# Chunks of 64 tokens and loads by token in a retention and feed-forward kernel

## The chip, the cores and the metric

The kernel runs on one core of a Trainium2 chip. The metric is the device time of one execution in microseconds (us). The profile is one execution, recorded by the hardware profiler.

## The reference

Retention over 4 sequences of 768 tokens, 8 heads, head size 64, then a feed-forward layer with a leaky activation over all 3072 tokens:

```python
for t in range(S):
    state = gamma[None, :, None, None] * state + np.einsum('bhd,bhe->bhde', k[:, :, t], v[:, :, t])
    y[:, :, t] = scale * np.einsum('bhd,bhde->bhe', q[:, :, t], state)
...
h = x @ w_in
g = np.maximum(h, 0.0) + alpha * np.minimum(h, 0.0)
return (g @ w_out).astype(np.float32)
```

`x` is y with its heads side by side (3072 x 512), `w_in` is 512 x 2048 and `w_out` 2048 x 512. Everything comes and goes in float32.

## The kernel before

**Blocks, units, loads.** The feed-forward layer works in six blocks of 512 tokens (n from 0 to 5). A block of retention is two units of 256 tokens and 8 heads (u from 0 to 11, three to a sequence). A unit is loaded as two parts (w = 2u and 2u + 1), each 4 heads by 256 tokens: three DMAs of 256 KB (k, q, v), in which a partition holds two neighbouring tokens of a head, 512 bytes in one piece (`load`, L151). `prep` (L183 to L212) scales k and q by powers of the decay on GpSimd into float16 (`scaled`, L191), casts v (L211), and from w = 8 on turns k and q by one DMA transpose (L204) into `kq`, with the head dimension on the partitions. For w = 0 to 7 TensorE does the turning.

**Retention in chunks.** Before the change a chunk is 128 tokens. Inside a chunk the products of q and k (scores, into PSUM) are masked on VectorE into float16 (`m2`) and multiplied with v ("inner", L360 in `inner`). What comes from earlier chunks is the product of q with a running state `tgs` ("carried", L340 in `carried`). The state is brought forward on VectorE by adding the chunk's sum of k times v (L511) and multiplying by the decay of 128 tokens (L513). All these matmuls use a quarter of the array each, 64 rows by 64 columns, four of them beside each other; their moving operand has 128 columns for scores, inner and carried, and 64 for the state sums (L481).

**Visits.** From block 2 on retention is done in visits of TensorE between matmuls of the feed-forward layer. `both(u_old, u_new)` (L425) does the last steps of an old unit and the first steps of a new one: scores of the new unit's second part into spare halves of banks (`low`, `sums`, L437), a small VectorE instruction that tells when they are through (`through`, L372), inner and half of carried for the old unit, a small ScalarE instruction (`word`, L374) that tells when these are through, scores of the first part, state sums, the other half of carried (it writes the bank that the other row half wrote before, so it waits for `word`), then on ScalarE the copy of y to `xT` (L498), and masks and states on VectorE.

**The order around them is written by hand.** For block n, `ffn1` (matmuls L557, 64 of them, activation on ScalarE L537 and VectorE L526) and `ffn2` (matmuls L582, four groups of 16, copies L596, stores L602) are generators; `tick(gen, m)` lets m matmuls go by. L754 to L774 interleave: two or four calls of `ahead()` in `ffn1`, then in `ffn2(n)` the visits. In block n = 1 there are three: (none, 4) after 8 matmuls, (4, 5) 28 later, (5, 6) 21 later. Then, 20 and 53 matmuls into `ffn2`: (6, 7) and (7, 8) at n = 2, (8, 9) and (9, 10) at n = 3, (10, 11) and (11, none) at n = 4. `ahead()` does `prep(w)` and then `load(w + 4)`, from w = 8 on.

**Queues.** Loads, transposes and stores are all issued by SyncE, in program order. GpSimd does casts and scalings in program order. `Banks` (L109) gives the order in which `ffn1` goes through the eight PSUM banks: f and p are two banks each that alternate, s and y pairs (S and Y their second halves). `ffn2` uses the f banks alone; `both` uses s, y and the p banks (`pa`, `pb`), and before the change an f bank for `low`.

Of the kernel before, what the change touches and what calls it, by code (L numbers as in the profile page):

```python
# [18 lines left out]
def kernel(  # L19
# [14 lines left out]

    nc = tc.nc
# [24 lines left out]
    for g in range(2):  # L60
        for x in range(2):
            for r in range(2):
                tab_np[64 * r : 64 * r + 64, 32 + 2 * g + x] = g64[4 * g + 2 * r + x] ** 128
    ALT = 48
# [8 lines left out]
    mi_np[:, 256:384] = np.eye(128)  # L73

# [9 lines left out]
    mask = mi[:, 0:256]  # L84
    ident = mi[:, 256:384]
# [59 lines left out]
    def load(w, which="kqv"):  # L145
        u, g, b, c3 = place(w)
        t = staged.setdefault(w, {})
        for nm in which:
            src = {"k": k, "q": q, "v": v}[nm]
            t[nm] = sbp.tile([128, 4, 2 * D], FP, tag=f"{nm}s", bufs=8, name=f"{nm}s{w}")  # L150
            nc.sync.dma_start(  # L151
                out=t[nm],
                in_=src[b, 4 * g : 4 * g + 4, TU * c3 : TU * c3 + TU, :].rearrange(
                    "h (p a) d -> p h (a d)", a=2
                ),
            )
# [26 lines left out]
    def prep(w, opening=False, k_on=None, q_on=None):  # L183
        u, g, b, c3 = place(w)
        t = staged.pop(w)
        kdq = sbp.tile([128, 2, 4, 2, D], F16, tag="kdq", bufs=8, name=f"kdq{w}")
        vx = sbp.tile([128, 4, 2, D], F16, tag="vx", bufs=8, name=f"vx{w}")
        kq = sbp.tile([128, 8, 128], F16, tag="kq", bufs=8, name=f"kq{w}")

        def scaled(eng, kind, src):  # L190
            eng.tensor_tensor(  # L191
                out=kdq[:, kind].rearrange("p z r d -> p r z d"),
                in0=src.rearrange("p (r x) (a d) -> p r (x a) d", a=2, x=2),
                in1=tab[:, 16 * kind + 8 * g : 16 * kind + 8 * g + 8]
                .rearrange("p (r z) -> p r z", r=2)
                .unsqueeze(3)
                .to_broadcast([128, 2, 4, D]),
                op=MULT,
            )
# [12 lines left out]
        prepped[w] = (kdq, kq, vx)  # L212
# [86 lines left out]

    def masked(w):  # L300
        kdq, kq, vx, sc = live[w]
        m2 = sbp.tile([128, 4, 2, 128], F16, tag="m2", bufs=4, name="m2")
# [8 lines left out]
    def new_state():  # L311
        return sbp.tile([128, 4, D], F16, tag="tg", bufs=8, name="tg")

    def state(w, cs=None):
        u, g, b, c3 = place(w)
        decay = tab[:, 32 + 2 * g : 34 + 2 * g].unsqueeze(2).to_broadcast([128, 2, D])
        for c in cs or chunks(w):
# [4 lines left out]
            if 2 * u + c + 1 not in tgs:  # L322
                tgs[2 * u + c + 1] = new_state()
            nc.vector.tensor_tensor(out=tgs[2 * u + c + 1][:, gs], in0=stv, in1=decay, op=MULT)

    def single(g, c, r):
        return slice(256 + 256 * c + 128 * r, 384 + 256 * c + 128 * r)

    def double(g, c, r):
        return slice(512 * c + 256 * g + 128 * r, 512 * c + 256 * g + 128 * r + 128)  # L330

    def carried(w, y, started, same, after=None, at=single):
        u, g, b, c3 = place(w)
        kq = live[w][1]
        for x in range(2):
            for r in range(2):
                c = r if same else 1 - r
                if c3 + c == 0:
                    continue
                ins = nc.tensor.matmul(  # L340
                    out=y[half(x), at(g, c, r)],
# [12 lines left out]
    def inner(w, y, started, at=single):  # L354
        u, g, b, c3 = place(w)
        vx, m2 = live[w][2:4]
        for r in range(2):
            for a in range(2):
                for c, x in DIAG:
                    nc.tensor.matmul(  # L360
                        out=y[half(x), at(g, c, r)],
# [63 lines left out]
    def both(u_old, u_new):  # L425
# [6 lines left out]
        def score(w, at):  # L432
            kq = prepped[w][1]
            for x in range(2):
                for a in range(2):
                    for r, c in DIAG:
                        last = nc.tensor.matmul(  # L437
                            out=at[r][x][half(c), 128 * a : 128 * a + 128],
                            lhsT=kq[half(r), 2 * x + a, half(c)],
                            rhs=kq[half(r), 4 + 2 * x : 6 + 2 * x, half(c)],  # L440
                            start=True,
                            stop=True,
                        )
            return last

        def masks(dst, src):
            nc.vector.tensor_tensor(  # L447
                out=dst.rearrange("p s a i -> p s (a i)"),
                in0=src.rearrange("p (s n) -> p s n", n=256),
                in1=mask.unsqueeze(1).to_broadcast([128, dst.shape[1], 256]),  # L450
                op=MULT,
            )

        if new:
            u, _, b, c3 = place(new[0])
            cs = chunks(new[0])
            low = ps("low", "fb" if flip["f"] else "fa")
            sums = [ps(f"sums{c}", "pa" if c == 0 else "pb") for c in range(2)]
            beside = [t[:, 256:512] for t in sums]
            there = through(score(new[1], ((low[:, 0:256], low[:, 256:512]), beside)))  # L460
            m2 = [sbp.tile([128, 4, 2, 128], F16, tag="m2", bufs=4, name="m2") for _ in new]
            masks(m2[1][:, 0:2], low)
# [8 lines left out]
        if new:  # L471
            sc = ps("sc", "s")
            score(new[0], [[sc[:, 512 * r + 256 * x :][:, 0:256] for x in range(2)] for r in range(2)])
            for w in new:
                kdq, kq, vx = prepped[w]
                for x in range(2):
                    for a in range(2):
                        for c, r in DIAG:
                            if c in cs:
                                at = 128 * (w % 2) + 64 * x  # L480
                                ins = nc.tensor.matmul(  # L481
                                    out=sums[c][half(r), at : at + 64],
                                    lhsT=kdq[half(c), 0, 2 * x + a, r, :],
                                    rhs=vx[half(c), 2 * r + x, a, :],
                                    start=(a == 0),
                                    stop=(a == 1),
                                )
                                if there is not None:
                                    behind(ins, there, "the other row half wrote this bank")
                                    there = None  # L490
        if old:
            for w in old:
                carried(w, y, started, False, done if w == old[0] else None, double)
# [4 lines left out]
            nc.scalar.activation(  # L498
                out=xT[n][:, 4 * i : 4 * i + 4].rearrange("p c r (i a) -> p (c r) i a", a=2),
                in_=y.rearrange("p (s a i) -> p s i a", a=2, i=64),  # L500
# [4 lines left out]
        if new:  # L505
            for c in range(2):
                masks(m2[1][:, 2 + c : 3 + c], beside[c])
            for c in cs:
                stv = sums[c][:, 0:256].rearrange("p (z e) -> p z e", e=D)
                if c3 + c > 0:  # L510
                    nc.vector.tensor_tensor(out=stv, in0=tgs[2 * u + c], in1=stv, op=ADD)  # L511
                tgs[2 * u + c + 1] = new_state()
                nc.vector.tensor_tensor(  # L513
                    out=tgs[2 * u + c + 1],
                    in0=stv,
                    in1=tab[:, 32:36].unsqueeze(2).to_broadcast([128, 4, D]),
                    op=MULT,
                )
            masks(m2[0], sc)
            for w, m in zip(new, m2):  # L520
                live[w] = [*prepped.pop(w), m]
# [171 lines left out]
    for w in range(2 * WB, 3 * WB):  # L693
        load(w)
# [42 lines left out]
    visit(6, 7, None, ("pb", "fa"))  # L737
    tick(gen, 4)
# [5 lines left out]
    more = [8]  # L744

    def ahead():
        w = more[0]
        if w < NW:
            prep(w)
            if w + WB < NW:  # L750
                load(w + WB)
            more[0] += 1

    for n in range(1, NBLK):  # L754
        gen = ffn1(n, "fyfpsYpS" if n > 1 else "spyfSpYf")
        for i in range(4 if n == 1 else 2):
            tick(gen, 14 if n == 1 else 20)
# [5 lines left out]
        if n + 1 < NBLK:  # L763
            tick(gen, 8)
            if n == 1:
# [39 lines left out]
```

## Time and profile before

| what | value |
| --- | --- |
| time, median of 3 runs | 210.86 us (210.62 to 211.15) |
| the profiled execution: its own time | 211.09 us |
| its span, first to last instruction | 209.1 us |
| TensorE matmuls busy | 201.5 us (96%), 2135 of them |
| VectorE, ScalarE, GpSimd busy | 123.2, 97.9, 72.8 us |
| granted TensorE clock | 0.998 |
| DMA moved | 38.27 MB in 64119 packets, 64.6% of 16 engines' span on SyncE's queue |

The profile's chain of waits tells which work ended last, step by step; its pieces are start, length, engine, name and line, and how many instructions were merged. The chain starts a matmul's piece where the one before has ended, so its pieces add up to the span. The groups give the busy time of a line, where the matmuls' modelled ends overlap. Queue and wait views tell what an engine or the DMA queue of SyncE waited for.

### The profile page before, as it was taken

Reading aid. Unit: us, or ns where it says so; the run is one execution under the profiler, and the core shown is the slowest. Engines: PE = TensorE matmul, PEld = TensorE weight load, DVE = VectorE, ACT = ScalarE, POOL = GpSimd, SP = SyncE. Lnnn points to the kernel's source line nnn. Section 1 sums busy time; section 2 is a strip of 40 time slices with the busy share of each in tenths; the row PEclk is TensorE's granted clock in tenths of the full one; section 3 lists DMA queues with packets and bytes.
Section 4 is the critical chain, followed back from the end, with each engine's and each line's share of the span. In section 5 each row is a group of like instructions: output and inputs, shape, how many; then the busy total and the mean of one; then the engine's idle time right before and its main releaser. Section 6 shows DMA issues by size and latency. Waiting matters only on the chain.

```text
span 209.1 us, 5197 instructions
## 1 busy us (share of the span) xinstructions
PE 201.5 (96%) x2135; PEld 101.5 (49%) x2135; DVE 123.2 (59%) x209; ACT 97.9 (47%) x166; POOL 72.8 (35%) x97
## 2 busy tenths in 40 slices
PE   7988999999999999999999999999999999999993
PEld 2565445445444555444555444545444544444452
DVE  2583886557588834888373688354888340588000
ACT  2572865174666122666233566233566123665121
POOL 0388798479927664345450054000000000000000
PEclk9999999999999999999999999999999999999999
DMA  6999999999999999799911399111410111100112
GB/s 179 307 286 345 389 389 383 371 312 306 358 254 253 298 252 202 248 233 265 266 71 74 104 235 211 53 56 56 122 31 0 50 53 50 53 0 0 50 55 96
DMA packets 64119, 38.27 MB, mean 183 GB/s; under 512 B 19152, under 2 KB 57568, under 8 KB 64096
## 3 DMA queue, kind: packets, MB, share of 16 engines
q1 hardware_dynamic: 63632, 37.69, 64.6%
q8 instruction: 16, 0.26, 0.5%
q10 hardware_dynamic: 464, 0.25, 0.5%
q14 instruction: 7, 0.06, 0.1%
HBM read 27.45 MB, written 6.29 MB: 161 GB/s over the span
## 4 chain that ended last, share of the span: by engine, by line
PE 88%; SPq 4%; DMA 3%; DVE 1%; ACT 1%; issue 1%; POOL 0%; DVEq 0%; ACTq 0%
PE hps L557 40%; PE ops L582 39%; SPq L151 4%; DMA wi<-in_moe_w_in_dram 3%; PE y L360 2%; PE y L340 2%; PE low L437 1%; PE sums L481 1%; PE sc L437 1%; PE trb L239 1%; DVE m L303 1%; ACT kq L245 0%; PE sc L267 0%; ACT os L596 0%; PE st L292 0%
## 5 line engine op out<-in xcount | busy, mean ns | idle before, releaser
L582 PE MATMUL ops<-wout,gt 128*128 128x512 f16 (+1 forms) x400 | 87.2, 371 | 0.3 <-ACT os L596 0.3
L526 DVE SCALAR_TENSOR_TENSOR gt<-hm,oma,hps 128x512 f16<-128x512 f32 x96 | 71.2, 747 | 26.4 <-ACT hm L537 16.7
L557 PE MATMUL hps<-xT,win 128*128 128x512 f16 (+1 forms) x392 | 84.8, 375 | 0.5 <-POOL win L181 0.5
L537 ACT ACTIVATE hm<-hps 128x512 f32<-128x512 f32 x96 | 57.0, 597 | 24.9 <-PE hps L557 24.5
L557 PEld LDWEIGHTS <-win 128*128 128x128 f16 x392 | 38.0, 98 | 45.3 <-POOL win L181 0.7
L582 PEld LDWEIGHTS <-gt 128*128 128x128 f16 x400 | 37.9, 98 | 41.4 <-issue 0.6
L596 ACT ACTIVATE os<-ops 128x512 f32<-128x512 f32 (+2 forms) x25 | 14.2, 576 | 46.6 <-PE ops L582 46.6
L191 POOL TENSOR_TENSOR kdq<-ks,tab 128x512 f16<-128x512 f32 x19 | 19.8, 1042 | 38.6 <-DMA ks<-in_k_dram 30.5
L191 POOL TENSOR_TENSOR kdq<-qs,tab 128x512 f16<-128x512 f32 x22 | 23.2, 1054 | 9.4 <-DMA ks<-in_k_dram 7.8
L447 DVE TENSOR_TENSOR m<-low,mi 128x512 f16<-128x512 f32 x8 | 5.5, 686 | 24.8 <-issue 24.0
L245 ACT ACTIVATE kq<-trb 128x512 f16<-128x512 f16 (+1 forms) x12 | 8.6, 736 | 10.7 <-PE trb L239 10.6
L211 POOL CAST vx<-vs 128x512 f16<-128x512 f32 x16 | 9.8, 610 | 3.5 <-PE y L360 3.0
L181 POOL CAST win<-wi 128x512 f16<-128x512 f32 x16 | 9.8, 613 | 2.8 <-DMA wi<-in_moe_w_in_dram 2.3
L181 POOL CAST wout<-wo 128x512 f16<-128x512 f32 x16 | 9.6, 613 | 3.3 <-DMA wo<-in_moe_w_out_dram 3.1
L303 DVE TENSOR_TENSOR m<-sc,mi 128x1024 f16<-128x1024 f32 x8 | 9.8, 1222 | 0.8 <-PE sc L267 0.4
L498 ACT ACTIVATE xT<-y 128x1024 f16<-128x1024 f32 x8 | 8.2, 1023 | 3.3 <-PE y L340 3.3
L447 DVE TENSOR_TENSOR m<-sc,mi 128x1024 f16<-128x1024 f32 x8 | 9.7, 1214 | 0.0
L340 PE MATMUL y<-kq,tg 64*64 64x128 f16 x160 | 8.5, 224 | 0.5 <-ACT word L374 0.4
L360 PE MATMUL y<-m,vx 64*64 64x128 f16 x384 | 8.3, 218 | 0.2 <-DVE m L303 0.2
L219 PE MATMUL trb<-ones 128*128 128x512 f16 (+1 forms) x21 | 6.5, 434 | 1.5 <-DVE word L624 1.4
L374 ACT ACTIVATE word<-word 1x1 f32<-1x1 f32 x11 | 2.2, 201 | 12.1 <-PE y L340 12.1
L600 DVE COPY os<-ops 128x128 f32<-128x128 f32 x1 | 0.3, 291 | 12.8 <-ACT os L596 12.8
(39 smaller groups left out, 99.5 us busy)
## 6 DMA issues: line engine op xcount, KB each, us to landing
ks<-in_k_dram SPq DMA_DIRECT2D x24, 256.0 KB, 4.6
qs<-in_q_dram SPq DMA_DIRECT2D x24, 256.0 KB, 4.7
vs<-in_v_dram SPq DMA_DIRECT2D x24, 256.0 KB, 4.8
out_dram<-os SPq DMA_DIRECT2D x23, 256.0 KB, 2.2
wi<-in_moe_w_in_dram SPq DMA_DIRECT2D x16, 256.0 KB, 6.1
wo<-in_moe_w_out_dram SPq DMA_DIRECT2D x16, 256.0 KB, 5.3
kq<-kdq SPq DMA_TRANSPOSE x16, 4.9
mi<-mi_const ACTq DMA_DIRECT2D x1, 128.0 KB, 3.5
```

Source lines behind the costliest of these rows:

```text
L181: nc.gpsimd.tensor_copy(out=dst, in_=t)
L191: eng.tensor_tensor(out=kdq[:, kind].rearrange("p z r d -> p r z d"), in0=src.rearrange("p (r x) (a d) -> p r (x a) d", a=2, x=2), in1=tab ...
L211: nc.gpsimd.tensor_copy(out=vx, in_=v_in)
L303: nc.vector.tensor_tensor(out=m2.rearrange("p s a i -> p s (a i)"), in0=sc.rearrange("p (s n) -> p s n", n=256), in1=mask.unsqueeze(1).to_ ...
L340: ins = nc.tensor.matmul(out=y[half(x), at(g, c, r)], lhsT=tgs[2 * u + c][half(r), 2 * g + x, :], rhs=kq[half(r), 4 + 2 * x : 6 + 2 * x, h ...
L360: nc.tensor.matmul(out=y[half(x), at(g, c, r)], lhsT=vx[half(c), 2 * r + x, a, :], rhs=m2[half(c), 2 * r + x, a, :], start=(c, x) not in s ...
L447: nc.vector.tensor_tensor(out=dst.rearrange("p s a i -> p s (a i)"), in0=src.rearrange("p (s n) -> p s n", n=256), in1=mask.unsqueeze(1).t ...
L526: nc.vector.scalar_tensor_tensor(out=gt[:, ft, lo:hi], in0=hm, scalar=oma_sb[:, ft : ft + 1], in1=hps, op0=MULT, op1=ADD,)
L537: nc.scalar.activation(out=hm, in_=hps, func=RELU, bias=0.0, scale=-1.0)
L557: nc.tensor.matmul(out=hpss[ft][:, 128 * lo : 128 * hi], lhsT=w_in_all[:, hp, 128 * ft : 128 * ft + 128], rhs=xT[n].rearrange("p (g t) r i ...
L582: nc.tensor.matmul(out=opss[tq], lhsT=gt[:, ft, 128 * tq : 128 * tq + 128], rhs=w_out_all[:, ft, at], start=(ft == 0), stop=(ft == NFT - 1),)
L596: nc.scalar.activation(out=os_sb, in_=opss[tq][:, cut], func=COPY, bias=0.0, scale=1.0)
```

## The change

From w = 8 on (block 2) a chunk is 64 tokens. A part w is then 128 tokens of all 8 heads instead of 256 tokens of 4 heads; a partition holds one token of 8 heads, so a load is made of 256-byte pieces (`w < NPE` keeps the old form, NPE is 8). Scores, inner, carried and sums all have moving operands of 64 columns. A unit has four states instead of two; the decay is applied after every second. `scaled` is two GpSimd instructions of 256 columns instead of one of 512. Scores of both parts go to one PSUM pair, so `low`, its memset and the halves beside `sums` are gone, and one mask of 1024 columns follows. The two visits of an old unit without a new one run three feed-forward matmuls (`mid`) between the halves of carried. `prep` of parts 8 and 9 is done ahead of `ffn1(1)`, and `ahead()` is `prep(w)` with `load(w + 2)`, from w = 10 on. Unit 6 is no longer begun in the visit of unit 5, but by a visit of its own in `ffn2(2)`. The ticks and `ffn1`'s bank order for n > 1 change.

```diff
@@ load @@
+            if w < NPE:
...
+            else:
+                at = TU * c3 + 128 * g
+                nc.sync.dma_start(
+                    out=t[nm].rearrange("p a (b d) -> p (a b) d", b=2),
+                    in_=src[b, :, at : at + 128, :].rearrange("h p d -> p h d"),
+                )
@@ scaled, in prep @@
+            if w >= NPE:
+                for i in range(2):
+                    at = 64 + 8 * kind + 4 * i
+                    eng.tensor_tensor(
+                        out=kdq[:, kind, 2 * i : 2 * i + 2].rearrange("p x r d -> p r x d"),
+                        in0=src[:, 2 * i : 2 * i + 2].rearrange("p r (x d) -> p r x d", x=2),
...
@@ both: inner, half of carried @@
         if old:
             y = ps("y", "y")
             started = set()
             for w in old:
-                inner(w, y, started, double)
+                vx, m2 = live[w][2:4]
+                for r in range(2):
+                    for g in range(2):
+                        for c, x in DIAG:
+                            at = 512 * r + 256 * (w % 2) + 64 * (2 * g + x)
+                            nc.tensor.matmul(
+                                out=out_of(y, w, x, c, g, r),
+                                lhsT=vx[half(c), 2 * g + r, x, :],
+                                rhs=m2[half(c), at : at + 64],
...
             for w in old:
-                last = carried(w, y, started, True, None, double)
+                last = carry(w, y, True)
             done = through(last, nc.scalar)
+            if not new:
+                mid()
@@ both: scores and sums @@
+            js = range(3 if c3 == NUS - 1 else 4)
             sc = ps("sc", "s")
-            score(new[0], [[sc[:, 512 * r + 256 * x :][:, 0:256] for x in range(2)] for r in range(2)])
+            for w in new:
+                kq = prepped[w][1]
+                for z in range(4):
+                    for r, c in DIAG:
+                        at = 512 * r + 256 * (w % 2) + 64 * z
+                        nc.tensor.matmul(
+                            out=sc[half(c), at : at + 64],
+                            lhsT=kq[half(r), z, half(c)],
+                            rhs=kq[half(r), 4 + z, half(c)],
...
@@ both: states @@
+            for j in js:
+                t, c = divmod(j, 2)
+                stv = sums[c][:, 256 * t : 256 * t + 256].rearrange("p (z e) -> p z e", e=D)
+                first, last = c3 + j == 0, c == 1
+                to = tgs[4 * u + j + 1] = new_state()
+                if not first:
+                    nc.vector.tensor_tensor(
+                        out=stv if last else to, in0=tgs[4 * u + j], in1=stv, op=ADD
+                    )
+                elif not last:
+                    nc.vector.tensor_copy(out=to, in_=stv)
+                if last:
...
@@ the order by hand @@
-    for w in range(2 * WB, 3 * WB):
+    for w in (8, 9, 10):
         load(w)
...
+    prep(8)
+    prep(9)
+    load(11)
     tick(gen, 4)
     within(7)
...
-        gen = ffn1(n, "fyfpsYpS" if n > 1 else "spyfSpYf")
-        for i in range(4 if n == 1 else 2):
-            tick(gen, 14 if n == 1 else 20)
+        gen = ffn1(n, "fspyfSpY" if n > 1 else "spyfSpYf")
+        for i in range(2):
+            tick(gen, 10 if n == 1 else 20)
             ahead()
...
-            tick(gen, 8)
-            if n == 1:
+            early = n < 3
+            tick(gen, 2)
+            if early:
                 both(None, u0)
             ahead()
             ahead()
-            tick(gen, 28 if n == 1 else 12)
+            tick(gen, 24 if early else 12)
             both(u0, u0 + 1)
-            tick(gen, 21 if n == 1 else 33)
-            both(u0 + 1, u0 + 2 if 2 * u0 + 4 < NW else None)
+            tick(gen, 26 if early else 28)
+            more_units = n > 1 and 2 * u0 + 4 < NW
+            both(u0 + 1, u0 + 2 if more_units else None, lambda: tick(gen, 3))
```

More of the change, by code (lines that the diff above doesn't have):

```diff
@@ L63 @@
                 tab_np[64 * r : 64 * r + 64, 32 + 2 * g + x] = g64[4 * g + 2 * r + x] ** 128
+    for h in range(H):
+        tab_np[:, 64 + h] = g64[h] ** (127.0 - np.arange(128))
+        tab_np[:, 72 + h] = scale * g64[h] ** (np.arange(128) + 1.0 - 128.0)
     ALT = 48
@@ L190, in scaled @@
         def scaled(eng, kind, src):
+            if w >= NPE:
[4 more added lines that the diff above has]
+                        in0=src[:, 2 * i : 2 * i + 2].rearrange("p r (x d) -> p r x d", x=2),
+                        in1=tab[:, at : at + 4]
+                        .rearrange("p (r x) -> p r x", r=2)
+                        .unsqueeze(3)
+                        .to_broadcast([128, 2, 2, D]),
+                        op=MULT,
+                    )
+                return
             eng.tensor_tensor(
@@ L298, in state_sums, with new_m2 @@
                         )
+    def new_m2():
+        return sbp.tile([128, 4, 2, 128], F16, tag="m2", bufs=3, name="m2")
     def masked(w):
         kdq, kq, vx, sc = live[w]
-        m2 = sbp.tile([128, 4, 2, 128], F16, tag="m2", bufs=4, name="m2")
+        m2 = new_m2()
         nc.vector.tensor_tensor(
@@ L311, in new_state @@
     def new_state():
-        return sbp.tile([128, 4, D], F16, tag="tg", bufs=8, name="tg")
+        return sbp.tile([128, 4, D], F16, tag="tg", bufs=12, name="tg")
     def state(w, cs=None):
@@ L321, in state, with carried @@
                 nc.vector.tensor_tensor(out=stv, in0=tgs[2 * u + c][:, gs], in1=stv, op=ADD)
[L322 to L332, printed above, removed]
+            to = 2 * u + c + 1 if 2 * u + c + 1 < NPE else 2 * NPE
+            if to not in tgs:
+                tgs[to] = new_state()
+            nc.vector.tensor_tensor(out=tgs[to][:, gs], in0=stv, in1=decay, op=MULT)
+    def carried(w, y, started, same, after=None):
         u, g, b, c3 = place(w)
@@ L340, in carried @@
                 ins = nc.tensor.matmul(
-                    out=y[half(x), at(g, c, r)],
+                    out=y[half(x), 256 + 256 * c + 128 * r : 384 + 256 * c + 128 * r],
                     lhsT=tgs[2 * u + c][half(r), 2 * g + x, :],
@@ L352, in carried, with inner @@
         return ins
-    def inner(w, y, started, at=single):
+    def inner(w, y, started):
         u, g, b, c3 = place(w)
@@ L360, in inner @@
                     nc.tensor.matmul(
-                        out=y[half(x), at(g, c, r)],
+                        out=y[half(x), 256 + 256 * c + 128 * r : 384 + 256 * c + 128 * r],
                         lhsT=vx[half(c), 2 * r + x, a, :],
@@ L423, in visit, with both @@
             state(w_new, cs)
-    def both(u_old, u_new):
+    def both(u_old, u_new, mid=None):
         old = [] if u_old is None else [2 * u_old, 2 * u_old + 1]
         new = [] if u_new is None else [2 * u_new, 2 * u_new + 1]
[L432 to L462, printed above, removed]
@@ new lines, in out_of, with carry @@
+        def out_of(y, w, x, c, g, r):
+            at = 512 * c + 256 * (w % 2) + 64 * (2 * g + r)
+            return y[half(x), at : at + 64]
+        def carry(w, y, same, after=None):
+            u, t, b, c3 = place(w)
+            kq = live[w][1]
+            for z in range(4):
+                for r in range(2):
+                    c = r if same else 1 - r
+                    if c3 + 2 * t + c == 0:
+                        continue
+                    ins = nc.tensor.matmul(
+                        out=out_of(y, w, z % 2, c, z // 2, r),
+                        lhsT=tgs[4 * u + 2 * t + c][half(r), z, :],
+                        rhs=kq[half(r), 4 + z, half(c)],
+                        start=False,
+                        stop=True,
+                        skip_group_check=True,
+                    )
+                    if after is not None:
+                        behind(ins, after, "the other row half wrote this bank")
+                        after = None
+            return ins
@@ L466, in both @@
             for w in old:
-                inner(w, y, started, double)
+                vx, m2 = live[w][2:4]
+                for r in range(2):
+                    for g in range(2):
[5 more added lines that the diff above has]
+                                rhs=m2[half(c), at : at + 64],
+                                start=(c, x) not in started,
+                                stop=False,
+                                skip_group_check=True,
+                            )
+                            started.add((c, x))
@@ L468, in both @@
             for w in old:
-                last = carried(w, y, started, True, None, double)
+                last = carry(w, y, True)
             done = through(last, nc.scalar)
+            if not new:
+                mid()
         if new:
+            u, _, b, c3 = place(new[0])
+            js = range(3 if c3 == NUS - 1 else 4)
             sc = ps("sc", "s")
-            score(new[0], [[sc[:, 512 * r + 256 * x :][:, 0:256] for x in range(2)] for r in range(2)])
+            for w in new:
+                kq = prepped[w][1]
+                for z in range(4):
+                    for r, c in DIAG:
[3 more added lines that the diff above has]
+                            lhsT=kq[half(r), z, half(c)],
+                            rhs=kq[half(r), 4 + z, half(c)],
+                            start=True,
+                            stop=True,
+                        )
@@ L474, in both @@
+            sums = [ps(f"sums{c}", "pa" if c == 0 else "pb") for c in range(2)]
             for w in new:
                 kdq, kq, vx = prepped[w]
[L476 to L490, printed above, removed]
+                for z in range(4):
+                    for c, r in DIAG:
+                        if 2 * (w % 2) + c in js:
+                            at = 256 * (w % 2) + 64 * z
+                            nc.tensor.matmul(
+                                out=sums[c][half(r), at : at + 64],
+                                lhsT=kdq[half(c), 0, z, r, :],
+                                rhs=vx[half(c), 2 * (z // 2) + r, z % 2, :],
+                                start=True,
+                                stop=True,
+                            )
@@ L491, in both @@
         if old:
             for w in old:
-                carried(w, y, started, False, done if w == old[0] else None, double)
+                carry(w, y, False, done if w == old[0] else None)
                 live.pop(w)
@@ L498, in both @@
             nc.scalar.activation(
-                out=xT[n][:, 4 * i : 4 * i + 4].rearrange("p c r (i a) -> p (c r) i a", a=2),
-                in_=y.rearrange("p (s a i) -> p s i a", a=2, i=64),
+                out=xT[n][:, 4 * i : 4 * i + 4].rearrange("p s r (c i) -> p (s r) c i", c=2),
+                in_=y.rearrange("p (c s i) -> p s c i", c=2, i=64),
                 func=COPY,
@@ L505, in both @@
         if new:
[L506 to L521, printed above, removed]
+            m2 = new_m2().rearrange("p s a i -> p (s a i)")
+            nc.vector.tensor_tensor(
+                out=m2.rearrange("p (s i) -> p s i", i=64),
+                in0=sc.rearrange("p (s i) -> p s i", i=64),
+                in1=mask64.unsqueeze(1).to_broadcast([128, 16, 64]),
+                op=MULT,
+            )
+            for j in js:
[4 more added lines that the diff above has]
+                if not first:
+                    nc.vector.tensor_tensor(
+                        out=stv if last else to, in0=tgs[4 * u + j], in1=stv, op=ADD
+                    )
+                elif not last:
+                    nc.vector.tensor_copy(out=to, in_=stv)
+                if last:
+                    nc.vector.tensor_tensor(
+                        out=to,
+                        in0=stv,
+                        in1=tab[:, 32:36].unsqueeze(2).to_broadcast([128, 4, D]),
+                        op=MULT,
+                    )
+            for w in new:
+                live[w] = [*prepped.pop(w), m2]
     gts = {}
@@ L737, with ahead @@
     visit(6, 7, None, ("pb", "fa"))
+    more = [10]
+    def ahead():
+        w = more[0]
+        if w < NW:
+            prep(w)
+            if w + 2 < NW:
+                load(w + 2)
+            more[0] += 1
+    prep(8)
+    prep(9)
+    load(11)
     tick(gen, 4)
```

21 lines of the change are left out of this document (7 added, 14 removed).

## The prediction

> **What bounds the kernel now.** I read the page's busy times and slices first, then its chain of waits, then the chain in order of time.
>
> ```profile
> PE 201.5 (96%) x2135; PEld 101.5 (49%) x2135; DVE 123.2 (59%) x209; ACT 97.9 (47%) x166; POOL 72.8 (35%) x97
> ...
> PE   7988999999999999999999999999999999999993
> ...
> DMA  6999999999999999799911399111410111100112
> ...
> PE 88%; SPq 4%; DMA 3%; DVE 1%; ACT 1%; issue 1%; POOL 0%; DVEq 0%; ACTq 0%
> ```
>
> TensorE is the bound: full in every slice from the sixth on, and 88% of the chain. A gain must come out of TensorE's own stream. The DMA row is full up to the slice that ends at 84 us, again from 89 to 105 and from 120 to 131 us: there the loads have no slack to give. The chain in order of time, at three places:
>
> ```profile
> 82.41 0.17 PE low L437
> 82.59 0.05 PE low L437
> 82.65 0.05 PE low L437
> 82.70 0.05 PE low L437
> 82.76 0.45 PE y L360 x32
> 83.21 0.11 PE y L340 x8
> 83.32 0.22 PE sc L437 x16
> 83.54 0.25 PE sums L481 x32
> 83.79 0.20 PE y L340 x8
> 83.99 1.62 PE ops L582 x7
> 85.61 13.81 PE hps L557 x64
> ...
> 174.33 0.57 PE y L360 x32
> 174.91 0.14 PE y L340 x6
> ...
> 175.13 0.21 ACT word L374
> 175.34 0.04 issue
> 175.38 0.31 PE y L340 x8
> ```
>
> This is one whole visit, 1.58 us, with no pause between its groups, and the last visit, in which TensorE waits for ScalarE. Rates: a feed-forward matmul is 13.81 / 64 = 0.216 us. A quarter-array matmul with 128 columns is 0.45 / 32 = 14 ns (inner) and 0.22 / 16 = 14 ns (scores). One with 64 columns is 0.25 / 32 = 7.8 ns (sums). The first 16 scores take 0.34 where the second take 0.22, and inner takes 0.57 where it comes first, against 0.45: entering a visit costs 0.12 us. The way out shows in the feed-forward piece behind a visit: 33 matmuls in 7.23 us are 0.11 over 33 x 0.216. The nine visits begin at 69.01, 76.25, 82.41, 103.74, 112.47, 134.66, 143.41, 165.59 and 174.33 us and take 1.09, 1.52, 1.58, 1.50, 1.58, 1.52, 1.57, 1.52 and 1.36 us: 13.24 us in all.
>
> **The change, TensorE.** Per unit: scores 32 of 128 columns become 32 of 64, inner the same; carried 16 of 128 become 32 of 64; sums stay at 64. In the chain's terms:
>
> - Visit with old and new unit: entry 0.12, inner 32 x 7.8 = 0.25, first half of carried 16 x 7.8 = 0.125, scores 0.25, sums 0.25, second half 0.125 and some 0.05 for the wait for `word` (before, 0.03 to 0.09 over the first half's 0.11): 1.17 us. That wait's cover, scores and sums, was 0.22 + 0.25 = 0.47 and becomes 0.50: it stays. Before: 1.50 to 1.58.
> - New unit only: 0.12 + 0.25 + 0.25 = 0.62. Before 1.09, of which the chain shows 0.08 of waiting for VectorE's memset and sums at 0.44 for 0.25; the memset is gone.
> - Old unit only: 0.12 + 0.25 + 0.125, then three feed-forward matmuls, which are work to be done anyway and hide `word`, then a second entry and half: 0.12 + 0.125. Together 0.75, and one way out more (0.11). Before 1.36, with 0.33 of pause.
>
> There are now 2 of the second kind (n = 1 and, new, n = 2), 6 whole ones and 2 of the third (n = 1 and 4): 2 x 0.62 + 6 x 1.17 + 2 x 0.75 = 9.76. Ways out rise from 9 to 12 (10 visits and 2 splits): + 3 x 0.11 = 0.33. So 10.09 for 13.24: **-3.15 us**. The feed-forward matmuls are the same in number.
>
> The trace has no score, inner or carried with 64 columns. Bounds: 7.8 ns (sums, the same 64 by 64 form with one weight load each) and 14 ns (inner). I take 7.8: what differs is the source, not the form. At 14 ns a whole visit would take 1.77, and 2 x 0.82 + 6 x 1.77 + 2 x 1.14 + 0.33 = 14.87: 1.63 us slower.
>
> **The change, what lies beside.** VectorE: a whole visit's masks and states were 0.69 + 2 x 0.42 + 1.21 + 3 or 4 x 0.42, and become 1.21 + 4 to 6 x 0.42: no more. Is it in time? Its last activation ends 1.41 us after `ffn1` ends (its run ends at 68.69, `ffn1` at 67.28); mask and six state steps (0.45 apart) end at 1.41 + 1.21 + 2.70 = 5.3. The next visit's carried comes at 26 x 0.216 + 0.73 + 0.37 = 6.7. 1.4 us spare. The visit entered after 2 matmuls needs the bank pairs back: at n = 2 the p bank of the fifteenth tile is free at 1.41 - 0.86 = 0.55 and its sums begin at 0.43 + 0.12 + 0.25 = 0.80. Spare 0.25; if missed, up to 0.6 us a visit.
>
> ScalarE: the same `word` and `xT` copies. The copy (1.02 us) ends before the next `ffn1`, with 9 matmuls (1.9 us) left at n = 1 and 12 at n = 2.
>
> GpSimd: two instructions of 256 columns for one of 512 (1.04 us). Bounds 0.52 and 1.04 each; I take 0.6, near the linear end, since a cast of 512 takes 0.61. Even at 1.04 four scalings and a cast are 4.8 us a part, 19 us a block of 31.
>
> SyncE's queue and the DMAs: 48 loads change from 512 pieces of 512 bytes to 1024 of 256. What each transpose stands behind: those of parts 8 and 9 move ahead of the fourth store of block 0 and of all but nine of the loads of parts 8 to 11; each later load now stands behind the transpose of the part two before it, which waits for GpSimd. The tight one is part 11's: the second visit of n = 1 needs it 0.62 + 0.11 + 26 x 0.216 + 0.50 = 6.8 us after 67.28, at 74.1 us. Between 46.7 us (the load of v 7, issued at 41.42 with 5.3 us to landing) and its own landing the queue has 15 loads, 4 stores of 0.65, 4 transposes of 1.15 (spacings of landings in the trace) and some 1.2 us of others: 55.1 + 15 x, with x the spacing of loads. At 512-byte packets x is 0.75 to 0.86 (350 to 305 GB/s). A 256-byte load packet is not in the trace. Packets take 27 ns at 512 bytes and 84 at 2048, so 17 by the line through both; the transposes' 256-byte packets have a median of 18. Bounds for x: 0.75 (bytes alone) and 1.72 (27 ns each, twice the packets). I take 1.0 to 1.15, by the 18 ns row: 70 to 72.4 us, in time by 2 to 4. The break is at x = 1.27. Later parts have more: 12 and 13 landed at 76.6 and 81.9 before, and are now needed 0.4 us into `ffn2(2)`, near 98 us; 16 and 17, the last to meet a full row, landed by 103.8, have 12 loads of 0.3 us more between and are needed at 110.
>
> The Trainium skill, "DMA: Bandwidth & Descriptors", Specifications, wants at least 512 bytes for line rate and tells of a read-modify-write below; that would be the upper bound for x. The same page, "Why small descriptors are slow (HBM only)", counts 256/32 + 3 = 11 cycles for a 256-byte descriptor; by that an estimate for two against one of 512 (19 cycles) is 1.16, x = 0.9 to 1.0, and no stall. No load of the trace tells which holds.
>
> **Sum.** 211.09 (the profiled execution, span 209.1 and 2.0 around it) - 3.15 = 207.94. The median before is 0.23 under that execution, so a median after would be 207.7. I say **207.8**.
>
> **Rivals.**
>
> 1. *Slower: loads of 256 bytes are late.* With x = 1.5 part 11's transpose lands at 77.6, 3.5 us late: 211.3. With 1.72 it is 80.9: 6.8 us late, 214.6. Centre 213; it decides from x = 1.27, between there and 1.48 the gain is only eaten. For it: the full DMA row, and part 13's transpose, which before landed at 81.9 for a visit at 82.4. Against: the 18 ns, and that 6 loads of parts 12 to 15 have moved from ahead of this transpose to behind it.
> 2. *Entered too early.* Sums of the two new-only visits wait for activations, 0.6 us each: 209.0. Against: the spare 0.25 above.
> 3. *64 columns cost as much as 128* (the reading is that 7.8 ns is a matter of what stands around sums): 212.6. Against: each group of four sums in the visit at 82 us follows at the same distance.
> 4. *The change does not do what it says:* the feed-forward's matmuls take up the freed time. They run at 0.216 us everywhere, with no wait to fill: nothing speaks for it, and it gets under 0.01.
>
> **How the numbers follow.** Forecast 0.78 (207.2 to 208.5: restart and way out after 64 columns, 0.02 each way a visit, and 0.3 of measuring); rival 2 0.06; the gain partly eaten by loads (208.5 to 211) 0.05; rival 1 in full 0.08; rival 3 0.03. The range goes from 207.1 over rival 2 to 209.2: with the least of the eaten gain that is 0.85 of the cases by this count, and 0.15 is left out above. A measurement here tells 0.3% (0.63 us) from no change. Faster: 0.78 + 0.06 + 0.03 = 0.87; same 0.03; slower 0.10.
>
> **What would show it.** Whole visits of 1.2 us; scores, inner and carried at 7.8 ns; no wait for a transpose at the second visit of n = 1 (74 us); the chain still TensorE from 17 us on; `word` no longer in the chain. Wrong: a transpose or GpSimd in the chain between 67 and 80 us, 256-byte load packets of 20 ns or more, or sums waiting for L526 two matmuls into `ffn2`.

## The result and the profile after

The changed kernel takes 208.45 us (median of 4 runs, 208.25 to 209.17) against 210.91 us before (4 runs, 210.62 to 211.15): a ratio of 0.989, 95% interval 0.9862 to 0.9918. The forecast was 207.8 us, with 207.1 to 209.2 around it. The profiled execution took 208.65 us, with a span of 206.9. Each ratio compares only runs within 1.5% of the fastest of their kernel, so it need not be the quotient of the medians beside it.

The page after, the lines that answer to those of before: busy times, TensorE's and the DMAs' slices, the chain's shares, and the group of the new GpSimd scalings.

```profile
PE 198.8 (96%) x2287; PEld 99.1 (48%) x2287; DVE 120.0 (58%) x195; ACT 97.6 (47%) x166; POOL 77.6 (37%) x129
...
PE   7888899999999999999999999999999999999993
...
DMA  6999999999999999999982399982320021100112
...
PE 86%; DMA 6%; SPq 4%; DVE 1%; ACT 1%; issue 0%; POOL 0%; DVEq 0%
...
L207 POOL TENSOR_TENSOR kdq<-ks,tab 128x256 f16<-128x256 f32 x32 | 18.9, 612 | 43.1 <-DMA ks<-in_k_dram 36.7
```

TensorE is still the bound: it has 152 more matmuls and 2.7 us less busy time. The DMA row is full for longer (up to the slice that ends at 103 us), and nothing of it reaches the chain behind the opening. (In this execution the chain goes by a load of weights up to 22.14 us, and TensorE holds it from 22.9 on, not from 17.) `word` (L398) is gone from it. A scaling of 256 columns takes 0.61 us (forecast 0.6).

The chain in order of time (start, length, engine, name and line, instructions merged), at the first three visits and at the last whole one:

```profile
68.03 0.38 PE sc L514 x32
68.40 0.27 PE sums L528 x32
68.67 5.29 PE ops L637 x24
73.95 0.37 PE y L491 x32
74.33 0.14 PE y L469 x14
74.46 0.32 PE sc L514 x31
74.78 0.30 PE sums L528 x19
...
75.29 5.72 PE ops L637 x26
81.01 0.38 PE y L491 x32
...
81.52 0.75 PE ops L637 x3
82.27 0.25 PE y L469 x16
...
162.87 0.38 PE y L491 x32
...
164.05 6.15 PE ops L637 x28
```

The first piece of a visit holds the way in (0.12 us). The new-only visit takes 0.65 us (68.03 to 68.67), the whole ones 1.34 (73.95 to 75.29) and 1.18 (162.87 to 164.05), the split one 0.51 and 0.25 on either side of its three feed-forward matmuls. In the same terms, the ten visits take 0.65, 1.34, 0.76, 0.71, 1.30, 1.26, 1.22, 1.19, 1.18 and 0.76 us: 10.37. The nine of before took 13.24. With 0.33 for three more ways out that is 13.24 - 10.37 - 0.33 = 2.54 us gained. From the first matmul of `ffn1(1)` to the last group of `ffn2`, the trace shows 152.36 us before and 149.79 after: 2.57 us less. **The whole gain is in the visits.** This stretch is what the experiments below are compared by, since the opening ahead of it, in which the change leaves TensorE's work as it was, ended anywhere from 51.8 to 54.5 us in the profiled executions of this study. The stretch of the changed kernel was 149.64 in a second execution (r_changed) and 149.90 with one wait more in six visits (e7_wait), so differences of 0.15 us say nothing.

### The profile page after: what moved, and what is told of

It reads as the page before. It is cut to its first block, busy times and chain, and to the rows that moved or that the text cites. A ratio compares the mean times of both kernels' runs of the same rounds, so it can differ in the third digit from the quotient of the medians.

```text
span 206.9 us, 5523 instructions
## 1 busy us (share of the span) xinstructions
PE 198.8 (96%) x2287; PEld 99.1 (48%) x2287; DVE 120.0 (58%) x195; ACT 97.6 (47%) x166; POOL 77.6 (37%) x129
## 4 chain that ended last, share of the span: by engine, by line
PE 86%; DMA 6%; SPq 4%; DVE 1%; ACT 1%; issue 0%; POOL 0%; DVEq 0%
PE ops L637 40%; PE hps L612 38%; SPq L158 4%; DMA wi<-in_moe_w_in_dram 3%; DMA vs<-in_v_dram 3%; PE y L491 1%; PE sc L514 1%; PE sums L528 1%; PE y L469 1%; PE trb L265 1%; DVE m L332 1%; PE y L384 1%; ACT kq L271 0%; PE sc L293 0%; ACT os L651 0%
## 5 line engine op out<-in xcount | busy, mean ns | idle before, releaser
L207 POOL TENSOR_TENSOR kdq<-ks,tab 128x256 f16<-128x256 f32 x32 | 18.9, 612 | 43.1 <-DMA ks<-in_k_dram 36.7
L207 POOL TENSOR_TENSOR kdq<-qs,tab 128x256 f16<-128x256 f32 x32 | 18.9, 613 | 0.8 <-DMA qs<-in_q_dram 0.7
L398 ACT ACTIVATE word<-word 1x1 f32<-1x1 f32 x11 | 2.2, 201 | 17.2 <-PE y L469 16.3
L217 POOL TENSOR_TENSOR kdq<-qs,tab 128x512 f16<-128x512 f32 x6 | 6.5, 1083 | 8.8 <-DMA ks<-in_k_dram 7.3
L426 ACT ACTIVATE xT<-y 128x512 f16<-128x512 f32 x8 | 4.8, 597 | 6.5 <-PE y L364 6.5
L217 DVE TENSOR_TENSOR kdq<-ks,tab 128x512 f16<-128x512 f32 x5 | 3.4, 689 | 5.3 <-DMA ks<-in_k_dram 5.3
```

The costliest lines, as they stand in the source:

```text
L207: eng.tensor_tensor(out=kdq[:, kind, 2 * i : 2 * i + 2].rearrange("p x r d -> p r x d"), in0=src[:, 2 * i : 2 * i + 2].rearrange("p r (x d ...
L217: eng.tensor_tensor(out=kdq[:, kind].rearrange("p z r d -> p r z d"), in0=src.rearrange("p (r x) (a d) -> p r (x a) d", a=2, x=2), in1=tab ...
```

## The experiments

"Matmul starts" below are the starts of single matmuls in the trace; a visit's excess is its time beyond the feed-forward matmuls, by those starts, with the ways in and out. In this measure the changed kernel's visits are 0.74, 1.44, 0.60 + 0.34, 0.80, 1.40, 1.35, 1.32, 1.28, 1.27 and 0.60 + 0.34 us. The kernel before, run beside each group of experiments, gave medians of 211.62 us (for e1_fused, e2_no_mid, e5_scores2 and e6_order_only), 211.67 (e3_512, e4_128, e7_wait) and 210.66 (e8_split_whole, e9_fused_late, r_changed).

### e1_fused: unit 6 begun in the visit of unit 5 again

```diff
-            early = n < 3
+            early = n == 1
-            more_units = n > 1 and 2 * u0 + 4 < NW
+            more_units = 2 * u0 + 4 < NW
```

> The changed kernel, but unit 6 is begun in the visit of unit 5 again, and block 2's ticks in ffn2 are those of block 3 (14, then 28). Theory (TensorE's stream is the bound and every visit of its own costs an entry, a way out and a split): the visits of unit 5 and 6 took 0.60 + 0.34 + 0.81 and the next two 1.40 + 1.35 us beyond the feed-forward matmuls; fused they are three whole visits of some 1.35, so about 0.45 us faster than the changed kernel: 208.0. Rival (unit 6 needs its own time, because part 13's transpose is late): in the changed kernel it landed at 81.2 us, and here its scores come near 81.5; if it comes later, TensorE waits for it in that visit and the time is 208.4 or more.

208.04 us (207.27 to 209.81), ratio 0.985 (0.9795 to 0.9904), not to be told from the changed kernel by time. The stretch tells more: 150.26 us, 0.47 over the changed kernel's. Its chain:

```profile
79.25 3.81 DMA kq<-kdq
...
83.10 0.32 PE sc L514 x16
```

The scores of unit 6 wait for part 13's transpose, which lands at 83.06; by the matmul starts TensorE stands for 0.86 us, and the visit saved pays back 0.39 of it. That the time came out at the first theory's 208.0 is thus no sign for it. So a visit of unit 6's own does buy something: it takes scores off a transpose that isn't there yet.

### e9_fused_late: the same, that visit 6 matmuls later

```diff
-            tick(gen, 26 if early else 28)
+            tick(gen, 32 if early else 28)
```

> Unit 6 is begun in the visit of unit 5 again, as in the run with the two fused, but that visit comes 6 feed-forward matmuls later, 1.3 us. In that run the visit waited 0.86 us for part 13's transpose, and no other visit lost anything. If that wait is all that spoke against it: no wait, visits of 12.10 - 0.86 = 11.24 us against 11.60 in the changed kernel, a stretch of 149.4 us and a time 0.4 us under the changed kernel's. Rival: with 6 matmuls left behind the visit the copy of y on ScalarE (1.02 us) comes too late for the next block's first layer, which then waits 0.2 to 0.8 us at its start: a stretch of 149.6 to 150.2 us, no gain.

208.16 us (207.83 to 210.42), ratio 0.9889 (0.9843 to 0.9935); the stretch is 150.01 us, within the rival's. Its chain, beginning behind that visit's scores (DVE is VectorE):

```profile
84.21 1.23 DVE m L551
...
87.71 0.44 DVE tg L569
...
88.19 1.90 PE hps L612 x8
```

The visit took 1.37 us and waited for no transpose. But eight matmuls into the next block's first layer, at its third tile, TensorE stands for 0.65 us by the matmul starts. The order of banks for n > 1 begins f, s, p: the third tile takes a p bank, in which the visit's state sums lie, and the chain puts the wait down to mask and states on VectorE, which let go of it at 88.15 us. ScalarE's copy of y, which I had expected to be late, ended at 85.77 us, just ahead of the layer's first matmul at 85.82. So the rival's price came out (a wait of 0.2 to 0.8 us at the next layer), by another engine. The visit has little room on either side; no place between the two was run.

### e2_no_mid: no feed-forward matmuls inside the old-only visits

```diff
-            if not new:
-                mid()
```

> The changed kernel without the three feed-forward matmuls between the halves of carried in the two visits without a new unit. Theory: the wait for ScalarE's word comes back, 0.33 us of pause each, and an entry and a way out of 0.23 go: about 0.25 us a visit by the raw starts (0.52 for 0.27), 0.5 us slower, 208.9. Rival (the split costs what it hides): no difference beyond 0.2 us.

208.87 us (208.23 to 209.06), ratio 0.9869 (0.9817 to 0.9921), stretch 150.61 us: 0.82 over the changed kernel's. The two visits take 1.44 and 1.30 us for 0.95. The chain shows `word` again:

```profile
81.25 0.21 ACT word L398
...
81.51 0.32 PE y L469 x16
```

The split is worth 0.42 us a visit, more than I had expected, way in and out already paid.

### e3_512 and e4_128: the loads in pieces of 512 and of 128 bytes

```diff
-  out=t[nm].rearrange("p a (b d) -> p (a b) d", b=2), in_=src[b, :, at : at + 128, :] ...
+  out=t[nm], in_=src[b, 4*g : 4*g+4, TU*c3 : TU*c3+TU, :].rearrange("h (p a) d -> p h (a d)", a=2)   # e3_512
+  out=t[nm].rearrange("p a (b d) -> p (a b) d", b=4), in_=src[0:2, :, at : at + 128, 0:32] ...      # e4_128
```

> The changed kernel with the loads from part 8 on in 512-byte pieces as before (the tokens then stand in other places, so the output is another; bytes, DMAs and work are the same). Theory (the loads are hidden): the same time within 0.3 us, with landings of loads 0.75 us apart instead of 0.9. Rival (256-byte loads take something of the gain, by waits or by slowing TensorE's visits while the DMAs are busy): faster by 0.3 to 0.6 us, and the visits at 74 and 105 us shorter.

> The changed kernel with the loads from part 8 on in 128-byte pieces, 2048 to a load (it reads other elements, as many bytes; the output is another). Theory by the queue: landings of loads 1.2 to 1.8 us apart; with the break at 1.27 part 11's transpose comes late for the visit at 74 us; at 1.2 nothing is lost, at 1.8 up to 8 us. It shows how far the changed kernel is from the edge that the prediction named. Rival (the waits go by GpSimd's chain, not by the queue's rate): no more than 1 us slower.

With 512 bytes: 207.85 us (207.19 to 208.54), ratio 0.9816 (0.9764 to 0.9868). The loads land 0.76 us apart instead of 0.9, and the stretch is 149.80 us, the changed kernel's to 0.01. The visits at 74 and 105 us are 0.07 us shorter, as the rival said, but so they are in r_changed, where the loads are as they were; and e7_wait, run beside it with 256-byte loads, came to a ratio of 0.982 too. At 256 bytes the loads are hidden whole.

With 128 bytes: 218.70 us (215.78 to 219.93), ratio 1.0228 (1.0153 to 1.0303). Loads land 1.2 to 2.3 us apart and part 11's transpose at 78.75 us for a visit at 72.2. Its chain, and the stretches of its trace (length; busy us and instructions of PE, PEld, DVE, ACT, POOL; the granted TensorE clock; the DMAs' share; GB/s):

```profile
73.56 5.20 DMA kq<-kdq
...
78.80 0.43 PE sc L514 x13
```

```profile
72.00:80.00 8.00, 2.14 (x123) 1.69 (x122) 0.72 (x1) 0.28 (x2) 2.98 (x5) 0.86 0.89 150
80.00:86.00 6.00, 6.00 (x18) 2.26 (x17) 2.10 (x5) 1.54 (x2) 2.98 (x5) 0.62 1.07 176
```

This is rival 1 at its place: 6.3 us of standing still at the second visit of n = 1. And it costs more than the wait. After it the granted clock is 0.62, and about 12 feed-forward matmuls start 0.427 us apart instead of 0.216: 2.4 us more. The Trainium skill, "TensorE: Matmul & The Clock Gate", What's actually happening, tells of half the clock after an idle window of about 3.4 us; this run agrees, at 6.3 us idle and twice the time a matmul.

### e5_scores2: every score computed twice

```diff
-            for w in new:
+            for w in [*new, *new]:
                 kq = prepped[w][1]
```

> The changed kernel with the scores of each visit computed twice into the same place (the same result): 32 more matmuls of 64 columns in each of 8 visits. Array theory: 7.8 ns each, 0.25 us a visit, 2.0 us slower, 210.5, and the second pass as fast as the first. Supply theory (long runs of 64 columns outrun the supply of instructions): 10 ns or more each, 2.6 us or more slower, 211.1 or above, with uneven spacing of starts that grows along the run. Rival that 64 columns cost as 128: 14 ns, 3.6 us, 212.

212.31 us (210.28 to 213.28), ratio 1.0027 (0.9982 to 1.0073), stretch 153.58 us. The time is what the rival of 14 ns forecast (212), but by another sum. The 32 extra matmuls cost a visit 0.22 to 0.38 us, 0.292 in the mean: 9.1 ns each, far from 14, and between the 7.8 of the array theory and the 10 of the supply theory. So **64 columns cost what sums cost, and a little more in a long run**. In eight visits that is 2.3 of the 3.8 us. Most of the rest is one pause of 1.28 us:

```profile
76.58 1.28 issue
77.86 4.71 PE ops L637 x21
```

This pause lies between feed-forward matmuls, and "issue" means that nothing shown was waited for. Packets of 16 KB on the instruction queue start at 75.41 and 79.53 us around it, with the DMAs full. That instructions came late is my reading; no run tested it.

### e6_order_only: the kernel before, with the new order of visits

The chunks and loads of before, with the moved `prep` and loads, the early visits and the split.

> The kernel before with the change's order alone: ticks, bank order, the split with three matmuls, unit 6 in a visit of its own, prep of parts 8 and 9 ahead, load of the part two later; chunks and loads stay as they were. Theory (the gain is in the 64 columns): ten visits of the old cost, 2 x 1.09 + 6 x 1.55 + 2 x 0.91 + 3 x 0.11 = 13.6 for 13.24 us, so 0.4 us slower than before: 211.3. Rival (the gain is in the order and the earlier transposes): near the changed kernel, 208.5.

212.47 us (211.35 to 213.46), ratio 1.0039 (1.0001 to 1.0078), stretch 154.27 us: 1.9 longer than before, where I had expected 0.4. The first visit, entered after two matmuls, takes 2.29 us instead of 1.19. Its chain there:

```profile
66.56 0.76 DVE gt L528
...
67.36 0.21 PE low L437
```

`low` needs a bank that the first layer's last activation frees, and the TensorE stream meets it. The order alone loses; it needs the small chunks, whose scores fit into one bank pair. The small chunks with the old order were not run.

### e7_wait: a VectorE wait, long over, ahead of the sums of whole visits

```diff
+        early_word = nc.vector.memset(warm[0:1], 0.0) if old and new else None
...
+                            if early_word is not None:
+                                behind(ins, early_word, "a wait that is long over")
```

> The changed kernel with one more wait in each of the six visits with an old and a new unit: the first state sum waits for a VectorE memset issued when the visit begins, which is done long before. Wait theory (a wait in the run of 64-column matmuls costs TensorE some 0.1 us even when what it waits for is long over, because the instructions behind it come late): the four visits that had no such wait ahead of the sums (112, 133, 140 and 163 us) grow by 0.1 us each, 0.3 to 0.5 us in all. Contention theory (the early visits are longer because the DMAs are busy then): no change in any visit.

208.05 us (207.61 to 208.27), ratio 0.982 (0.9781 to 0.9858). The six visits change by +0.02, -0.07, +0.01, 0.00, +0.01 and +0.04 us. A wait that is over is not what makes whole visits long; my theory that it was falls. The starts show why: in the four visits that had no such wait, the first sum now comes 60 to 62 ns behind the last score, where it came 8 behind, but the sums after it go in quick groups of four again instead of one by one. The pause is paid back, which fits a limit in how fast instructions come.

### r_changed: the changed kernel once more

> The changed kernel as it is, once more, beside the kernel before on the same chip. 208.4 us and a ratio of 0.987 by the result; its stretch from the first matmul of the second block's first layer to the last group of the second layer 149.8 us, visits of 0.74, 1.43, 0.60 + 0.34, 0.80, 1.40, 1.35, 1.32, 1.28, 1.27 and 0.60 + 0.34 us. A visit that comes out more than 0.05 us otherwise was not a property of the program.

208.60 us (207.20 to 210.16), ratio 0.9889 (0.9843 to 0.9935), stretch 149.64 us. The visits come out as they were, to 0.01 us, but for two whole ones of blocks 1 and 2: 1.36 and 1.33 us for 1.44 and 1.40. So 0.07 us on each of these is a matter of the execution, and the rest is of the program.

### e8_split_whole: three feed-forward matmuls inside the whole visits too

```diff
-            if not new:
+            if mid:
                 mid()
...
-            both(u0, u0 + 1)
+            both(u0, u0 + 1, lambda: tick(gen, 3))
```

> Three feed-forward matmuls go between the first half of carried and the scores in the six whole visits too. A run of small matmuls with no pause costs, by the visits of an old unit alone (0.603 us for 48, 0.344 for 16), 7.9 ns each and 0.22 for way in and out. So 48 cost 0.60 and the other 72 to 80 cost 0.79 to 0.85: 1.39 to 1.46 us a whole visit. Theory that the instruction supply falls behind after some 50 matmuls in a row, and catches up during feed-forward matmuls: all six take 1.39 to 1.50 us, within 0.1 of each other, and the stretch is 150.2 to 150.7 us. Rival, that the excess of each visit (0.26, 0.23, 0.18, 0.09, 0.11, 0.10 us over its clean length) belongs to what it works on or to what runs beside it: they take 1.65, 1.62, 1.57, 1.55, 1.57, 1.56 us, and the stretch is 151.3 us.

208.96 us (207.74 to 210.50), ratio 0.9923 (0.9892 to 0.9954), stretch 150.57 us. The six whole visits take 1.45, 1.47, 1.45, 1.50, 1.47 and 1.45 us, where they spread from 1.27 to 1.44 before. The chain at the second visit, which had been 1.44:

```profile
74.06 0.38 PE y L491 x32
...
74.56 0.75 PE ops L637 x3
75.32 0.38 PE sc L514 x32
75.69 0.19 PE sums L528 x20
```

The first half runs at its clean rate, 0.60 us for 48 by the matmul starts; the second, 0.85 for 72, is 0.06 above it (at 7.9 ns each and 0.22 for the ways in and out it would be 0.79). The rival, 1.55 to 1.65 for a whole visit, is out. What the visits of the changed kernel have over 7.9 ns a matmul is then a matter of long runs of small matmuls, as the theory of the supply said, and not of what each visit works on. One reservation: the split also puts scores and sums 0.85 us later, so a wait for a bank would vanish too. The waits view names none there, but no run separates the two.

## Why the prediction was nearly right

- **TensorE's own stream is the bound and the gain comes out of it:** right. Visits and stretch agree to 0.03 us.
- **The visits, -3.15 us:** right in mechanism, too large by 0.6; measured -2.54 in the prediction's terms. This is the term that was mis-sized. Old-only visits were 0.76 for 0.75. New-only ones were 0.65 and 0.71 for 0.62. The six whole ones were 1.18 to 1.34, 1.25 in the mean, for 1.17: 0.47 us of the 0.61 missing.
- **The failing step in it: 7.8 ns for every 64-column matmul.** The rate is right for a short run. In matmul starts, groups of four follow each other 31.6 ns apart (7.9 ns each) in the new-only visit at 68 us, for all of its 64. In a whole visit of 120 to 128 this holds for some 50 to 60; then matmuls start one by one, 8.3 ns apart with steps of 17 and 25 ns between, so that 32 scores take 8.3 to 10 ns each. In the whole visits at 74 and 105 us the first sum also comes 131 and 126 ns behind the last score (60 and 61 in r_changed). The row I took the rate from, sums in the visit at 82 us of before, was 32 matmuls between others of 14 ns, and could not show this. My bounds (7.8 to 14) held; the choice at the lower end did not hold in long runs. That the limit is the supply of instructions is supported by e8_split_whole, by the paid-back pauses of e7_wait and, with its 9.1 ns, by e5_scores2; no view shows the supply itself. A pause of 60 ns goes with a wait ahead of the first sum, as e7_wait shows; what the two longer ones wait for stays open.
- **Sums of the second new-only visit** (98.8 us) start 0.06 us late, in every run of this order. That fits rival 2's bank, which I had put at a spare of 0.25 us or a loss of 0.6. VectorE let go of it at 98.93 us, 0.55 behind the layer as forecast; but by the matmul starts the sums were due at 99.02, so there was next to no spare. It wasn't tested by itself.
- **`word`'s wait of 0.05 us in whole visits:** it does not appear; second halves of carried follow sums at once. **The split** was sized rightly at 0.75 us, and e2_no_mid gives what it replaces.
- **Loads:** x was 0.9 us between loads with nothing in the way (mostly 0.87 to 0.97), by packets of 18 ns at 256 bytes, 27 at 512 and, in e4_128, 13 at 128. I took 1.0 to 1.15. Part 11's transpose landed at 72.10 us, within the forecast's 70 to 72.4, for 74.1. That it fell into the range is luck: with 0.9 the sum gives 68.6, and the other 3.5 us are pauses that the sum doesn't have. The 15 loads took 1.11 us each in the mean, and the transpose landed 2.51 us behind the load before it. From 46 to 104 us five landings came more than 1.9 us behind the one before, each of them 1.9 to 2.6 us behind the start of a packet of 16 KB on the instruction queue; no run tests whether that is the cause. Of the two rules of the Trainium skill, "DMA: Bandwidth & Descriptors", that the prediction cites, the count of cycles (Why small descriptors are slow (HBM only)) came out with its estimate of 0.9 to 1.0; the read-modify-write below 512 bytes (Specifications) shows no price in these runs. Rival 1 did not happen, but e4_128 shows that its mechanism and place were right.
- **Rival 3** (64 columns cost as much as 128) and **rival 4** fell, by the rows above.
- **The sum:** 211.09 - 2.58 (the stretch in the chain) + 0.32 (the opening ended later in this execution) + 0.06 (the end) - 0.24 (1.75 us around the span instead of 1.99) = 208.65. I gave 0.3 us to measuring; the opening alone moves by more than 2 us between executions.

## What to carry to other kernels

When a stream of one engine is the bound, sum its visits by their rows, but take a rate only for runs as long as the one it was read from: a rate from 32 small matmuls between larger ones did not hold for 120. Compare variants by a stretch of the trace that the edit touches, not by the whole time, when an untouched opening moves by more than the edit. An order tuned to one layout need not pay with another: the new order alone lost 1.9 us on the stretch, and with the smaller chunks the two together gained 2.6.

## What the runs showed of the hardware that was not expected

- Small matmuls keep their 7.9 ns for some 50 to 60 in a row, then fall to 8.3 to 10 ns; three feed-forward matmuls (0.65 us) restore them. A wait that is over puts 60 to 62 ns between two of them (e7_wait), and those behind it catch up.
- After 6.3 us of standing still TensorE's next 2.6 us of work took twice as long (clock 0.62 over 80 to 86 us).
- Loads of 256 KB in 256-byte pieces land 0.9 us apart (but for the pauses behind packets of the instruction queue, told above), in 512-byte pieces 0.76; in 128-byte pieces 1.2 to 2.3. Halving the piece from 512 to 256 costs 1.2 times, not twice.
- A pause of 1.28 us in the middle of plain matmuls, with nothing to wait for that the profile shows, between two packets of the instruction queue. The Trainium skill, "Runtime: NRT & Kernel Launch", Instruction fetch mechanics, says that instructions come in blocks of 16 KiB by a DMA queue, mostly hidden. The packets' size agrees; that this one was not hidden is only likely.
